# Folding w_phi into two projection weights by 120-row blocks, and copying three transposed tiles in two parts: a linear-attention and gated-MLP kernel

## The chip, the cores and the metric

The kernel runs on one core of a Trainium2 chip. The metric is the device time of one launch in microseconds (us). A core has five engines, each with its own queue that is worked in order: TensorE (PE in the profile, its weight loads PEld), VectorE (DVE), ScalarE (ACT), GpSimd (POOL) and SyncE (SP), which here only issues transfers (DMAs). TensorE writes to PSUM, eight banks of 512 fp32 columns; from there VectorE or ScalarE must copy results to SBUF. Engines wait for each other by semaphores.

## The reference

The input x has 2048 tokens of 640 features in bf16. It is layer-normalized, and the result xn feeds two branches whose outputs are added to x:

```python
xn = layernorm(x)                                   # 2048 x 640
q, k, v = split(xn @ wqkv)                          # 32 heads of 20 columns each
pq, pk  = q_h @ w_phi_h, k_h @ w_phi_h              # one 20x20 matrix per head
phi(p)  = concat(softmax(p), softmax(-p))           # 40 features per head
kv, z   = sum over tokens of phi_k x v, of phi_k
o       = (phi_q @ kv) / (phi_q . z + 1e-6)
out     = x + o @ wo + (silu(xn @ w1) * (xn @ w3)) @ w2   # w1, w3: 640 x 1536
```

## The kernel before

Tokens are worked in 16 tiles of 128, features in DC = 5 chunks of 128 partitions.

**An order made by a planner.** The code writes no order by hand. Each piece of work is a step of one of 14 streams (generators such as norms, transposes, fold_k, attention, mlps). A loop at lines 924 to 965 builds every stream's next step, asks when it could start by a table of modelled costs (`cost=` in the helpers, transfers in `commit`, lines 172 to 204), and commits the earliest. Each engine then gets its instructions in the order of commitment, and a wait for every dependency that it doesn't know to be met (`emit`). So a changed cost or size can also move steps that the edit doesn't touch. All instructions are recorded by one helper, so the profile shows them on line 102 (transfers on 114).

**The head of the program.** `first_loads` (414 to 431) issues the loads: x tiles 0 to 3 one by one, the v part of wqkv (wv), a third of w1 and w3, w_phi (phi_s), then k's part of wqkv transposed by the DMA (wqkT, one transfer of 640 rows by 640 columns), x tiles 4 to 15 in three transfers, and q's part of wqkv transposed. `consts` (434 to 443) makes the identity, zeros for idle products and the mask GM[128, 5, 32], which says for every chunk of 128 rows of w_phi (all heads stacked, 640 rows) to which head a row belongs. `consts_late` (445 to 450) makes three more constants on GpSimd after the statistics of tile 6: the mask M3 for the key-value sums, ones behind ekt, and a column of ones for every head in v2.

**Transposes.** TensorE transposes the normalized tiles 0 to 3 (`xn_transpose`, 519 to 528): five 128x128 products into PSUM, then copies to xnT. Tile 0 goes to two banks and is copied by ScalarE (three chunks) and VectorE (two). Tiles 1 to 3 go to one bank each and leave it in one copy of 640 columns, by whichever of ScalarE and VectorE the planner finds free (`evac`). Tiles 4 to 15 are transposed by DMAs. In between TensorE multiplies tiles 0 to 3 by wv: ten products of 320 columns a tile (`part`), two halves of five; the products of a tile need all its five chunks one after the other.

**The fold.** Since pq = xn (wq w_phi), the kernel multiplies w_phi into the weights once. `block_diag` (531 to 537) puts w_phi on the diagonal: for each chunk of 128 rows of w_phi it writes BDc[128, up to 8 heads x 20], one GpSimd product of 140 or 160 columns with the mask. 128 rows are 6.4 heads, so the chunks overlap in the heads at their edges. `fold_mm(which, dc, k)` (539 to 551) makes 128 rows of the folded weight Wkp (which = 1) or Wqp (0): for each chunk, the transposed weight block as the stationary operand and BDc as the moving one, split at column 320, which is where PSUM's second bank begins. That is six products for each dc, four of 140 columns and two of 80, and an evacuation of 640 columns. The five dc of k run after the first two groups of gate and up products, the five of q are strewn between the tiles 9 to 13 of attention.

**What follows.** k_tile (products with Wkp, two exponentials on ScalarE), v_tile, k_norm (VectorE sums, GpSimd scaling), the key-value sums, q_proj and its chain, `mlp` (ten products of 512 columns, tanh on ScalarE, two VectorE products) and `out_tile` at the end. PSUM banks are handed out in pairs (`banks`).

Of the kernel before, what the change touches and what calls it, by code (L numbers as in the profile page):

```python
# [9 lines left out]
D = 640  # L10
H = 32
# [9 lines left out]

ENGINES = ("PE", "ACT", "DVE", "POOL", "SP")
GRAN = 8


def heads_of_chunk(c):
    return (128 * c) // DH, (128 * c + 127) // DH


class _Op:  # L30
# [13 lines left out]
class _Program:  # L44
# [127 lines left out]
    def commit(self, ops):  # L172
        for o in ops:
            o.idx = len(self.ops)
            o.deps = self.find_deps(o)
            t = self.free[o.eng]
            for d in o.deps:
                t = max(t, d.end + (0.03 if d.eng == o.eng else 0.07))
            o.start = t
            if o.dma:  # L180
                self.free[o.eng] = t + 0.45
                if "T" == o.part:
                    self.free[o.eng] = t + (1.28 if o.cost < 5e5 else o.cost / 105e3)
                self.bus = max(self.bus, t + 0.5) + o.cost / (280e3 if o.part else 305e3)
                if o.part and o.cost > 5e5:
                    self.bus = max(self.bus, self.free[o.eng] + 1.0)
                o.end = self.bus + (1.5 if t < 1 else 1.6 if t < 3.5 or o.part and o.cost < 2e5 else 2.6)
# [62 lines left out]
def bass_parallel_sum__linear_kernel_hedgehog__glu_gated_swiglu__prompt_kernel(  # L250
# [29 lines left out]
    def new(name, shape, dtype, offset=None):  # L280
        size = mybir.dt.size(dtype)
        for n in shape[1:]:
            size *= n
        return P.sbuf(name, shape, dtype, region(size) if offset is None else offset)

    ident = new("ident", [128, 128], bf)
    GM = new("GM", [128, DC, H], bf)
    phi_s = new("phi_s", [128, DC, DH], bf)
    BDc = new("BDc", [128, DC, 8 * DH], bf)
    bst = new("bst", [128, T, 12], f32)  # L290
    mv = new("mv", [128, T, 2], f32)
    rstd = new("rstd", [128, T, 2], f32)
# [27 lines left out]
    ekt = new("ekt", [128, T * 2 * D + 48], bf, RE)  # L320
    hT3 = new("hT3", [128, FC, 512], bf, RE)
    w2_s = new("w2_s", [128, FC, D], bf, RE + 12288)
    eq = [new(f"eq{i}", [128, NG * 128], bf, (RKV, RE + 27648)[i // 2] + 2816 * (i % 2)) for i in range(4)]
    eqT = [new(f"eqT{i}", [128, NG, 128], bf, (RKV, RE + 27648)[i // 2] + 5632 + 2816 * (i % 2)) for i in range(4)]
    hT = [hT0, hT1, hT2, hT3]
# [3 lines left out]
    oT = new("oT", [128, DC, S], bf, RV)  # L329

    RW = region(12800)
    wqkT = new("wqkT", [128, 2 * DC, D], bf, RW)
    KVc = new("KVc", [128, NG * 64], bf, RW)
    half = new("half", [128, 2, 660], f32, RW + 1408)
    Sq = new("Sq", [128, 4, 72], f32, RW + 6688)
# [64 lines left out]
    x_t = A_x.rearrange("b (t p) d -> p (b t) d", p=128)  # L400
    out_t = out.rearrange("b (t p) d -> p (b t) d", p=128)
    wqkv_t = A_wqkv.rearrange("(c p) n -> p c n", p=128)
    phi_t = A_w_phi.rearrange("h d f -> (h d) f").rearrange("(c p) f -> p c f", p=128)
    w1_t = B_w1.rearrange("(c p) f -> p c f", p=128)
    w3_t = B_w3.rearrange("(c p) f -> p c f", p=128)

# [3 lines left out]

    def load_x(a, b):
        P.dma("SP", x_tok[:, a:b, :], x_t[:, a:b, :])

    def first_loads():
        def half_wv(eng, a):
            P.dma(eng, wv[:, :, a:a + 320], wqkv_t[:, :, 2 * D + a:2 * D + a + 320])

        P.dma("SP", x_tok[:, 0, 0:320], x_t[:, 0, 0:320])
        P.dma("ACT", x_tok[:, 0, 320:D], x_t[:, 0, 320:D])
        load_x(1, 2)  # L420
        load_x(2, 3)
        half_wv("ACT", 0)
        half_wv("SP", 320)
        load_x(3, 4)
        w13(0, 512)
        P.dma("SP", phi_s[:], phi_t)
        P.dma("SP", wqkT[:, DC:2 * DC, :], A_wqkv[:, D:2 * D], True)
        load_x(4, 8)
        load_x(8, 12)
        load_x(12, 16)  # L430
        P.dma("SP", wqkT[:, 0:DC, :], A_wqkv[:, 0:D], True)


    def consts():
        memset("DVE", t1[:, 2, :], 0.0)
        memset("DVE", warm[:], 0.0)
        act(warm[:], warm[:], ACT.Exp)
        memset("POOL", ident[:], 0.0)
        select(ident[:], 0, [[-1, 128]], 1, ALU.not_equal, 1.0)
        memset("POOL", GM[:], 1.0)  # L440
        select(GM[:], 0, [[128, DC], [-DH, H]], 1, ALU.is_ge, 0.0)
        select(GM[:], DH, [[-128, DC], [DH, H]], -1, ALU.is_gt, 0.0)
        memset("POOL", mhalf[:], -0.5)

    def consts_late():
        memset("POOL", M3[:, 0:3], 1.0)
        select(M3[:, 0:3], 0, [[-40, 3]], 1, ALU.is_ge, 0.0)
        select(M3[:, 0:3], 40, [[40, 3]], -1, ALU.is_gt, 0.0)
        memset("POOL", ekt[:, T * 2 * D:T * 2 * D + 48], 1.0)
        memset("POOL", v_heads(v2[:].rearrange("p t n -> p (t n)"))[:, :, :, DH], 1.0)  # L450


    def v_heads(a):
        return a.rearrange("p (g x) -> p g x", x=64)[:, :, 0:63].rearrange("p g (h c) -> p g h c", c=21)
# [58 lines left out]
    def idle(n, cols):  # L513
        z = t1[:, 2, :]
        for i in range(n):
            j = 7 - i if cols == 512 else 7
            mm(bank(j, cols), z[:, 0:128], z[:, 0:cols], True, True, cost=cols / 1200)

    def xn_transpose(t, k):
        dst = xnT[:, :, t * 128:(t + 1) * 128]  # L520
        for j, a, b in ((0, 0, 3), (1, 3, DC)) if t == 0 else ((0, 0, DC),):
            o = PSb[:, (k + j) * 1024:(k + j) * 1024 + 128 * (b - a)].rearrange("p (c n) -> p c n", n=128)
            for dc in range(a, b):
                tr(o[:, dc - a, :], x_tok[:, t, 128 * dc:128 * dc + 128])
            if t == 0:
                copy(("ACT", "DVE")[j], dst[:, a:b, :], o, 2)
            else:
                evac(dst, o)


    def block_diag():
        for c in range(DC):
            h0, h1 = heads_of_chunk(c)
            n = h1 - h0 + 1
            tt("POOL", BDc[:, c, 0:n * DH].rearrange("p (h k) -> p h k", k=DH),
               phi_s[:, c, :].unsqueeze(1).to_broadcast([128, n, DH]),
               GM[:, c, h0:h1 + 1].unsqueeze(2).to_broadcast([128, n, DH]), ALU.mult)

    def fold_mm(which, dc, k):
        first = [True, True]  # L540
        for e in range(DC):
            h0, h1 = heads_of_chunk(e)
            lo, hi = DH * h0, DH * (h1 + 1)
            for q in range(2):
                a, b = max(lo, 320 * q), min(hi, 320 * q + 320)
                if a < b:
                    mm(bank(k + q, b - a, a - 320 * q), wqkT[:, which * DC + e, 128 * dc:128 * dc + 128],
                       BDc[:, e, a - lo:b - lo], first[q], e == DC - 1 or (q == 0 and e == 2), True)
                    first[q] = False
        dst = (Wqp, Wkp)[which]  # L550
        evac(dst[:, dc, :].rearrange("p (b c) -> p b c", c=320), bank2(k, 320))


    def part(w, t, q, i, k, off=0):
# [172 lines left out]
    done = dict.fromkeys(("w", "ln", "t", "f", "k", "n", "kv", "v", "u", "qp", "qn", "qd", "q", "o", "h", "v0"), 0)  # L727

    def norms():
        yield lambda: (first_loads(), consts())  # L730
# [18 lines left out]
        yield lambda: ln_apply(3)  # L749
        done["ln"] = 4  # L750
        yield block_diag
        todo = []
        for t in range(4, T + 2, 2):
            if t == T or t > done["k"] + 8:
                for u in todo:
                    yield lambda u=u: ln_apply(u)
                    done["ln"] = u + 1
                todo = []
            if t == T:
                break  # L760
            while t > done["k"] + 8:
                yield None
            yield lambda t=t: ln_stats(t, 2)
            for u in todo:
                yield lambda u=u: ln_apply(u)
                done["ln"] = u + 1
            todo = [t, t + 1]
            if t == 6:
                yield consts_late

    def fold_k():
        for dc in range(DC):
            yield lambda dc=dc: fold_mm(1, dc, banks(2))
        done["f"] += 1
# [10 lines left out]
    def transposed(t):  # L785
        while done["ln"] <= t:
            yield None
        yield lambda: xn_transpose(t, banks(1 if t else 2))
        done["t"] = t + 1

    def transposes():
# [235 lines left out]
```

## Time and profile before

| | us |
|---|---|
| median of 3 runs | 268.59 (268.48 to 268.87) |
| the profiled execution: its time | 268.63 |
| its span, from the first to the last instruction | 266.9 |
| PE busy | 263.2 (99%) |
| DVE busy | 169.9 (64%) |
| POOL busy | 102.9 (39%) |
| ACT busy | 98.0 (37%) |

TensorE's clock is granted in full over the whole span (1.0). "Busy" says how long an engine had an instruction in work; matmuls overlap, so a busy TensorE can still be waiting for less than the length of a product. A row of the timeline gives the start, the length from the first start to the last end, the engine, the line, the instruction, what it writes and reads, its shapes and the count; in brackets stands idle time of the engine just before it and what ended it. A row with a count merges neighbours of like kind and takes its shape from the first. The chain is followed back from the last instruction, at each step to what released it.

### The profile page before, as it was taken

The numbers are of one execution on the slowest core, as the hardware profiler recorded it, in microseconds if no ns is written. First come the engines' busy times: TensorE is split into PE (matmuls) and PEld (weight loads), VectorE is DVE, ScalarE is ACT, GpSimd is POOL, SyncE is SP. The second block draws the span as 40 slices with busy tenths as digits, with TensorE's granted clock in tenths as the row PEclk, the third lists the DMA queues.
The fourth block names the chain that finished last, engine by engine and source line by source line (L and its number), as shares of the span: only waits on it lengthen the run. The fifth ranks groups of instructions, "written<-read, shape, count | busy, mean of one in ns | idle before, by whom it ended". The sixth has DMA issues, their size and how long they took to land.

```text
span 266.9 us, 4814 instructions
## 1 busy us (share of the span) xinstructions
PE 263.2 (99%) x1959; PEld 159.9 (60%) x1959; DVE 169.9 (64%) x292; ACT 98.0 (37%) x193; POOL 102.9 (39%) x144
## 2 busy tenths in 40 slices
PE   8999999999999999999999999999999999999996
PEld 4656677776754555555555544544577777777773
DVE  4559899997966779888888888988512121212112
ACT  5557989888224442443443344322100000000000
POOL 3317658999992344445555444420000000000000
DMA  7998795900095442445444553423212213131211
GB/s 214 295 315 166 178 192 111 311 1 2 6 333 64 79 79 44 92 83 101 79 81 79 97 84 78 92 50 77 49 52 74 75 54 95 52 98 49 88 37 49
DMA packets 63510, 27.73 MB, mean 104 GB/s; under 512 B 49920, under 2 KB 63488, under 8 KB 63488
## 3 DMA queue, kind: packets, MB, share of 16 engines
q1 hardware_dynamic: 62544, 26.90, 43.5%
q10 hardware_dynamic: 944, 0.52, 0.7%
q8 instruction: 15, 0.25, 0.4%
q14 instruction: 7, 0.06, 0.1%
HBM read 12.81 MB, written 2.62 MB: 58 GB/s over the span
## 4 chain that ended last, share of the span: by engine, by line
PE 98%; ACT 0%; DVE 0%; issue 0%
PE PS L102 98%; ACT xnT L102 0%; DVE xres L102 0%; DVE t L102 0%; DVE warm L102 0%
## 5 line engine op out<-in xcount | busy, mean ns | idle before, releaser
L102 PE MATMUL PS<-xnT,w_s 128*128 128x512 bf16 x480 | 107.7, 379 | 0.0
L102 PEld LDWEIGHTS PS<-xnT,w_s 128*128 128x128 bf16 x480 | 45.8, 98 | 51.0 <-ACT Wkp L102 0.2
L102 PE MATMUL PS<-w_s,hT 128*128 128x320 bf16 (+2 forms) x384 | 54.9, 299 | 0.0
L102 DVE TENSOR_TENSOR xres<-PS,xres 128x640 bf16<-128x640 f32 (+2 forms) x17 | 13.3, 785 | 59.9 <-PE PS L102 59.9
L102 ACT ACTIVATE th<-PS 128x512 f32<-128x512 f32 x48 | 29.3, 611 | 49.4 <-PE PS L102 49.4
L102 DVE SCALAR_TENSOR_TENSOR t<-th,PS 128x512 bf16<-128x512 f32 x48 | 32.5, 676 | 22.3 <-ACT th L102 22.3
L102 PEld LDWEIGHTS PS<-w_s,hT 128*128 128x128 bf16 x384 | 37.1, 98 | 15.1
L102 POOL TENSOR_TENSOR ekt<-ekt,rS 128x640 bf16<-128x640 bf16 x32 | 39.5, 1269 | 0.6 <-DVE rS L102 0.6
L102 ACT ACTIVATE eq<-PS 128x600 bf16<-128x600 f32 (+1 forms) x72 | 23.8, 424 | 29.7 <-PE PS L102 29.7
L102 DVE SCALAR_TENSOR_TENSOR hT<-t,PS 128x512 bf16<-128x512 bf16 x48 | 33.0, 687 | 1.7
L102 PE MATMUL PS<-wv,xnT 128*128 128x320 bf16 x160 | 24.5, 299 | 0.1
L102 PE MATMUL PS<-wo_s,oT 128*128 128x320 bf16 (+2 forms) x160 | 24.5, 299 | 0.0
L102 POOL TENSOR_TENSOR rq<-rq,Sq 128x32 f32<-128x32 f32 x16 | 4.0, 252 | 52.6 <-DVE rq L102 52.6
L102 PE MATMUL PS<-Wqp,xnT 128*128 128x512 bf16 (+1 forms) x160 | 24.2, 299 | 0.0
L102 PE MATMUL PS<-Wkp,xnT 128*128 128x320 bf16 x160 | 23.9, 299 | 0.0
L102 POOL TENSOR_TENSOR eq<-eq,rq 128x600 bf16<-128x600 bf16 (+1 forms) x32 | 22.6, 728 | 1.2
L102 DVE TENSOR_REDUCE S<-ekt 128x64 f32<-128x1280 bf16 x16 | 23.0, 1438 | 0.0
L102 ACT ACTIVATE ekt<-PS 128x640 bf16<-128x640 f32 x32 | 20.6, 709 | 4.8 <-PE PS L102 4.8
L102 POOL TENSOR_TENSOR half<-eq 128x660 f32<-128x660 bf16 x15 | 20.4, 1358 | 0.6 <-ACT eq L102 0.6
L102 PEld LDWEIGHTS PS<-wo_s,oT 128*128 128x128 bf16 x160 | 15.5, 98 | 6.5
L102 PEld LDWEIGHTS PS<-wv,xnT 128*128 128x128 bf16 x160 | 15.4, 98 | 6.3 <-ACT xnT L102 0.4
L102 PEld LDWEIGHTS PS<-Wqp,xnT 128*128 128x128 bf16 x160 | 12.9, 98 | 10.5
(56 smaller groups left out, 181.2 us busy)
## 6 DMA issues: line engine op xcount, KB each, us to landing
w_s<-in_B_w_dram SPq DMA_DIRECT2D x6, 640.0 KB, 6.3
xres<-in_A_x_dram SPq DMA_DIRECT2D x16, 160.0 KB, 2.5
out_dram<-xres SPq DMA_DIRECT2D x15, 160.0 KB, 1.8
x_tok<-in_A_x_dram SPq DMA_DIRECT2D x3, 640.0 KB, 6.4
w_s<-in_B_w_dram SPq DMA_DIRECT2D x1, 1920.0 KB, 8.4
wo_s<-in_A_wo_dram SPq DMA_DIRECT2D x1, 800.0 KB, 8.3
x_tok<-in_A_x_dram SPq DMA_DIRECT2D x3, 160.0 KB, 4.0
wv<-in_A_wqkv_dram ACTq DMA_DIRECT2D x1, 400.0 KB, 4.1
```

The source lines that it names most:

```text
L102: o = _Op(eng, lambda: m(*args, **kw), r, w, cost)
```

## The change

1. **The fold by heads.** w_phi and the transposed weights are cut into six blocks of whole heads: five of 120 rows (six heads) and one of 40 (two heads). Block g of k is loaded by a DMA of its own, transposing 128 columns from 640 + 120 g on, so neighbouring blocks overlap by eight columns that are not used; likewise for q. w_phi comes in two loads (600 and 40 rows). Each dc is folded by six products, five of 120 columns contracted over 120 rows and one of 40 over 40. They fill PSUM from column 32 of a pair of banks, so that four blocks end where the first bank ends, and the evacuation reads 640 columns in one piece.
2. **The masked weights** BD[128, 6, 120] are made by two GpSimd products (600 columns, 40 columns) with a mask of six columns, GM[128, 6].
3. **Tiles 1 to 3** are transposed into two banks each and leave them in two copies: ScalarE three chunks and two (tiles 1 and 2), VectorE two chunks and ScalarE three (tile 3).
4. **Constants at the head.** consts_late is gone; M3 and the ones behind ekt are made on GpSimd at the end of consts, the ones in v2 on VectorE.
5. k's blocks have a place of their own, in the region of ekt's later tiles; the planner counts a longer way to landing for small transposing loads from DRAM; fold_k waits in the planner until block_diag has been committed.

The order that the planner makes of it is, beside the edits themselves, the same on every engine up to the first gate products but for two things: eight instead of six v products stand between the transposes of tiles 1 and 2 (and 15 instead of 17 after those of tile 3), and v2's memset stands third on VectorE. From the key-value sums on, some groups of gate products stand at other places among the q tiles.

```diff
-    GM = new("GM", [128, DC, H], bf)
-    phi_s = new("phi_s", [128, DC, DH], bf)
-    BDc = new("BDc", [128, DC, 8 * DH], bf)
+    GM = new("GM", [128, 6], bf)
+    phi_s = new("phi_s", [128, 6, DH], bf)
+    BD = new("BD", [128, 6, 120], bf)
...
+    wkT = new("wkT", [128, 6, D], bf, RE + 20480)
...
-    wqkT = new("wqkT", [128, 2 * DC, D], bf, RW)
+    wqT = new("wqT", [128, 6, D], bf, RW)
...
-    phi_t = A_w_phi.rearrange("h d f -> (h d) f").rearrange("(c p) f -> p c f", p=128)
+    phi_t = A_w_phi.rearrange("h d f -> (h d) f")
...
+    def load_wT(which):
+        for g in range(6):
+            a = D * which + 120 * g
+            P.dma("SP", (wqT, wkT)[which][:, g, :], A_wqkv[:, a:a + 128], True)
...
-        P.dma("SP", phi_s[:], phi_t)
-        P.dma("SP", wqkT[:, DC:2 * DC, :], A_wqkv[:, D:2 * D], True)
+        P.dma("SP", phi_s[0:120, 0:5, :], phi_t[0:600, :].rearrange("(c p) f -> p c f", p=120))
+        P.dma("SP", phi_s[0:40, 5, :], phi_t[600:D, :])
+        load_wT(1)
         load_x(4, 8)
         load_x(8, 12)
         load_x(12, 16)
-        P.dma("SP", wqkT[:, 0:DC, :], A_wqkv[:, 0:D], True)
+        load_wT(0)
...
-        select(GM[:], 0, [[128, DC], [-DH, H]], 1, ALU.is_ge, 0.0)
-        select(GM[:], DH, [[-128, DC], [DH, H]], -1, ALU.is_gt, 0.0)
+        select(GM[:], 0, [[-DH, 6]], 1, ALU.is_ge, 0.0)
+        select(GM[:], DH, [[DH, 6]], -1, ALU.is_gt, 0.0)
         memset("POOL", mhalf[:], -0.5)
-
-    def consts_late():
+        memset("DVE", v_heads(v2[:].rearrange("p t n -> p (t n)"))[:, :, :, DH], 1.0)
         memset("POOL", M3[:, 0:3], 1.0)
         select(M3[:, 0:3], 0, [[-40, 3]], 1, ALU.is_ge, 0.0)
         select(M3[:, 0:3], 40, [[40, 3]], -1, ALU.is_gt, 0.0)
         memset("POOL", ekt[:, T * 2 * D:T * 2 * D + 48], 1.0)
-        memset("POOL", v_heads(v2[:].rearrange("p t n -> p (t n)"))[:, :, :, DH], 1.0)
...
+    PARTS = (((0, 0, 3, "ACT"), (1, 3, DC, "DVE")), ((0, 0, 3, "ACT"), (1, 3, DC, "ACT")),
+             ((0, 0, 3, "ACT"), (1, 3, DC, "ACT")), ((0, 0, 2, "DVE"), (1, 2, DC, "ACT")))
+
     def xn_transpose(t, k):
         dst = xnT[:, :, t * 128:(t + 1) * 128]
-        for j, a, b in ((0, 0, 3), (1, 3, DC)) if t == 0 else ((0, 0, DC),):
+        for j, a, b, e in PARTS[t]:
             o = PSb[:, (k + j) * 1024:(k + j) * 1024 + 128 * (b - a)].rearrange("p (c n) -> p c n", n=128)
             for dc in range(a, b):
                 tr(o[:, dc - a, :], x_tok[:, t, 128 * dc:128 * dc + 128])
-            if t == 0:
-                copy(("ACT", "DVE")[j], dst[:, a:b, :], o, 2)
-            else:
-                evac(dst, o)
+            copy(e, dst[:, a:b, :], o, 2)
...
     def block_diag():
-        for c in range(DC):
-            h0, h1 = heads_of_chunk(c)
-            n = h1 - h0 + 1
-            tt("POOL", BDc[:, c, 0:n * DH].rearrange("p (h k) -> p h k", k=DH),
-               phi_s[:, c, :].unsqueeze(1).to_broadcast([128, n, DH]),
-               GM[:, c, h0:h1 + 1].unsqueeze(2).to_broadcast([128, n, DH]), ALU.mult)
+        for n, a, b in ((120, 0, 5), (40, 5, 6)):
+            m = n // DH
+            o = BD[0:n, a:b, 0:n].rearrange("p c (h f) -> p c h f", f=DH)
+            tt("POOL", o, phi_s[0:n, a:b, :].unsqueeze(2).to_broadcast([n, b - a, m, DH]),
+               GM[0:n, 0:m].unsqueeze(1).unsqueeze(3).to_broadcast([n, b - a, m, DH]), ALU.mult)
 
     def fold_mm(which, dc, k):
-        first = [True, True]
-        for e in range(DC):
-            h0, h1 = heads_of_chunk(e)
-            lo, hi = DH * h0, DH * (h1 + 1)
-            for q in range(2):
-                a, b = max(lo, 320 * q), min(hi, 320 * q + 320)
-                if a < b:
-                    mm(bank(k + q, b - a, a - 320 * q), wqkT[:, which * DC + e, 128 * dc:128 * dc + 128],
-                       BDc[:, e, a - lo:b - lo], first[q], e == DC - 1 or (q == 0 and e == 2), True)
-                    first[q] = False
-        dst = (Wqp, Wkp)[which]
-        evac(dst[:, dc, :].rearrange("p (b c) -> p b c", c=320), bank2(k, 320))
+        c0 = k * 512 + 32
+        for g in range(6):
+            n = 120 if g < 5 else 40
+            mm(PS[:, c0 + 120 * g:c0 + 120 * g + n], (wqT, wkT)[which][0:n, g, 128 * dc:128 * dc + 128],
+               BD[0:n, g, 0:n], g in (0, 4), g in (3, 5), True)
+        evac((Wqp, Wkp)[which][:, dc, :], PS[:, c0:c0 + D])
...
-            if t == 6:
-                yield consts_late
...
-        yield lambda: xn_transpose(t, banks(1 if t else 2))
+        yield lambda: xn_transpose(t, banks(2))
```

More of the change, by code (lines that the diff above doesn't have):

```diff
@@ L23 @@
 GRAN = 8
-def heads_of_chunk(c):
-    return (128 * c) // DH, (128 * c + 127) // DH
 class _Op:
@@ L186, in commit @@
                     self.bus = max(self.bus, self.free[o.eng] + 1.0)
-                o.end = self.bus + (1.5 if t < 1 else 1.6 if t < 3.5 or o.part and o.cost < 2e5 else 2.6)
+                o.end = self.bus + (1.5 if t < 1 else 1.6 if t < 3.5 or o.part and o.cost < 2e5 and o.reads else 2.6)
             else:
@@ L725, in banks @@
         return min((k for k in range(0, 8, n) if k // 2 not in held), key=free_at)
-    done = dict.fromkeys(("w", "ln", "t", "f", "k", "n", "kv", "v", "u", "qp", "qn", "qd", "q", "o", "h", "v0"), 0)
+    done = dict.fromkeys(("w", "ln", "t", "f", "k", "n", "kv", "v", "u", "qp", "qn", "qd", "q", "o", "h", "v0", "bd"), 0)
     def norms():
@@ L751, in norms @@
         yield block_diag
+        done["bd"] = 1
         todo = []
@@ L767, in norms @@
             todo = [t, t + 1]
-            if t == 6:
-                yield consts_late
     def fold_k():
+        while not done["bd"]:
+            yield None
         for dc in range(DC):
```

## The prediction

> **What bounds the kernel now.** I read the page's span and chain shares first, then the chain in order of time, then the timeline of the places where the chain leaves TensorE.
>
> ```profile
> span 266.9 us, 4814 instructions
> PE PS L102 98%; ACT xnT L102 0%; DVE xres L102 0%; DVE t L102 0%; DVE warm L102 0%
> ```
> ```profile
> 7.52 0.47 PE PS L102 x5
> ...
> 8.01 0.71 ACT xnT L102
> 8.72 0.05 issue
> 8.77 10.90 PE PS L102 x90
> ...
> 19.67 244.91 PE PS L102 x1826
> ```
>
> The chain is TensorE's instruction stream: from 19.67 us to the end it is never left. It is left once in the stage that the change touches, at 8.01, for one ScalarE copy. So a change is worth what it takes out of TensorE's own stream, plus what it removes or adds in waits before about 20 us. Work moved on VectorE, GpSimd and SP counts only where TensorE comes to wait for it. Everything in the sum is against the profiled execution, 268.63 us (span 266.9 and 1.73 around it, which I leave alone); the median of the three runs shown is 268.59, so the two agree.
>
> **Term 1: the copies of tiles 1 to 3.** The timeline of TensorE, VectorE and ScalarE there (start, length, then the instruction and its count):
>
> ```profile
> 7.52 0.45 PE L102 MATMUL PS<-ident,x_tok 128*128 128x128 bf16 x5
> 7.81 1.27 PE L102 MATMUL PS<-wv,xnT 128*128 128x320 bf16 x6
> 8.94 0.45 PE L102 MATMUL PS<-ident,x_tok 128*128 128x128 bf16 x5
> 9.23 1.79 PE L102 MATMUL PS<-wv,xnT 128*128 128x320 bf16 x12
> 10.89 0.45 PE L102 MATMUL PS<-ident,x_tok 128*128 128x128 bf16 x5
> 11.18 2.47 PE L102 MATMUL PS<-wv,xnT 128*128 128x320 bf16 x17
> 13.49 4.48 PE L102 MATMUL PS<-xnT,w_s 128*128 128x512 bf16 x20
> ```
> ```profile
> 8.45 0.43 DVE L102 TENSOR_SCALAR x_tok<-x_tok,mv,rstd 128x640 bf16<-128x640 bf16 x1
> 10.38 0.45 DVE L102 TENSOR_SCALAR x_tok<-x_tok,mv,rstd 128x640 bf16<-128x640 bf16 x1 [0.66 <-POOL rstd L102]
> 6.11 0.49 ACT L102 ACTIVATE xnT<-PS 128x384 bf16<-128x384 bf16 x1 [0.16 <-PE PS L102]
> 8.01 0.70 ACT L102 ACTIVATE xnT<-PS 128x640 bf16<-128x640 bf16 x1 [1.41 <-PE PS L102]
> 8.69 0.72 ACT L102 ACTIVATE v<-PS 128x660 bf16<-128x660 f32 x1
> ```
>
> 17 products of 320 columns start between 11.18 and 13.49: 0.136 us each. After the transposes of tile 1, TensorE has five products of tile 0 left, 7.81 + 5 x 0.136 = 8.49. The sixth needs tile 1, whose copy ends at 8.71; it starts at 8.77, so 0.28 us are idle. Split, the first copy waits for three transposes instead of five: they start every (7.81 - 7.52)/5 = 0.06 us, so it starts about 0.11 earlier, at 7.90. It has the size of the 0.49 us row and ends at 8.39; with the 0.05 of issue, tile 1 can start at 8.44, before 8.49. The wait goes, by a margin of 0.05.
>
> What is late next is VectorE. The transposes of tile 2 need its normalization, done at 8.88, and those of tile 3 at 10.83; neither moves, so both groups stay at 8.94 and 10.89. But in the changed program eight products, not six, stand before 8.94 (8.49 + 3 x 0.136 = 8.90), and still twelve between 9.23 and 10.89. So 15 products are left after 11.18 instead of 17, and the gate products start 2 x 0.136 = **0.27 us earlier**, at 13.22.
>
> The other new copies must not be late in turn. From 384 and 640 columns (0.49, 0.70), 256 columns on ScalarE cost 0.39. Tile 1's second copy ends at 8.78 (needed after 9.23), the copy of v at 9.50, tile 2's two at 9.99 and 10.38 (needed at 9.23 + 7 x 0.136 = 10.18, and 10.59). Tile 3's last starts near 11.38 and ends at 11.87, needed at 11.18 + 7 x 0.136 = 12.13. Margins of 0.2 us: hidden. If the copies ran one after the other in the 0.70 of a whole copy each, the term would be nothing; that is its lower end.
>
> **Term 2: the fold's columns.** Sixty products of 140, 80 and 80 columns become fifty of 120 and ten of 40.
>
> ```profile
> 17.80 1.86 PE L102 MATMUL PS<-BDc,wqkT 128*128 128x140 bf16 x30
> 19.67 2.33 PE L102 MATMUL PS<-xnT,w_s 128*128 128x512 bf16 x10
> 45.73 0.48 PE L102 MATMUL PS<-BDc,wqkT 128*128 128x140 bf16 x6
> 46.05 1.52 PE L102 MATMUL PS<-Wkp,xnT 128*128 128x320 bf16 x10
> 68.48 3.96 PE L102 MATMUL PS<-v,ekt 128*128 128x63 bf16 x132
> 18.32 3.09 ACT L102 ACTIVATE Wkp<-PS 128x640 bf16<-128x640 f32 x5 [0.80 <-PE PS L102]
> ```
>
> A 512-column product takes (17.80 - 13.49)/20 = 0.2155 us and a 320-column one 0.136, so 0.000414 per column and 0.0035 over. A group before is 4 x 0.0615 + 2 x 0.0366 = 0.319; the row says 46.05 - 45.73 = 0.32. After: 5 x 0.0532 = 0.266 and one of 40 columns, which by columns would be 0.020, but 132 products of 63 and 42 columns start every 3.96/132 = 0.030 or a little less, so I take 0.029. That is 0.295, **0.024 less per group**. The five groups for q lie in the unbroken stretch: 0.12 us. The five for k are paced by ScalarE: 30 products from 17.80 end by columns at 17.80 + 5 x 0.32 = 19.40, yet the next product starts at 19.67, when ScalarE has emptied two banks. Only the first group's 0.024, before ScalarE's first copy, comes through; I count 0.03. Together **0.15 us**. Unknown is what contraction over 120 and 40 rows costs; every row here has 128. I take no difference; the ends are 0.33 gained (720 - 640 columns x 10 x 0.000414) and nothing.
>
> **Term 3: what feeds the fold.** One transposing load of 640 rows by 640 columns becomes six of 640 by 128, and w_phi comes in two loads.
>
> ```profile
> 0.80 1.34 SPq L114 DMA_DIRECT2D x_tok<-in_A_x_dram  x3
> 4.28 1.66 SPq L114 DMA_DIRECT2D phi_s<-in_A_w_phi_dram  x1
> 5.98 6.73 SPq L114 DMA_TRANSPOSE wqkT<-in_A_wqkv_dram  x1
> 12.76 1.67 SPq L114 DMA_DIRECT2D x_tok<-in_A_x_dram  x3
> 24.23 5.16 SPq L114 DMA_TRANSPOSE xnT<-x_tok  x4
> ```
> ```profile
> phi_s<-in_A_w_phi_dram SPq DMA_DIRECT2D x1, 25.0 KB, 7.8
> wqkT<-in_A_wqkv_dram SPq DMA_TRANSPOSE x1, 10.4
> xnT<-x_tok SPq DMA_TRANSPOSE x12, 2.7
> 12.00:14.00 2.00, 2.00 (x16) 1.35 (x14) 0.00 (x0) 1.03 (x2) 1.86 (x5) 1.00 1.27 290
> ```
>
> k's transposed weights land at 5.98 + 10.4 = 16.4, and the fold wants them at 17.80. After, the fold's first group wants its six blocks from 17.53 to 17.80. On SP, the second w_phi load costs about 1.34/3 = 0.45; then six issues like xnT's, which move as much each (160 KB): 5.16/4 = 1.29. The last is issued at 6.4 + 5 x 1.29 = 12.9 and lands 2.7 later, **15.6**: the early bound. The late one: w_phi lands at 12.1, and the five blocks needed 4.3 us from there; six at that rate need 5.2, **17.3**. Both are in time, by 0.5 us at the worst. The loads of x tiles 4 to 15 move from 12.76 to about 14.2; their first consumer, the statistics of tile 4, is VectorE work at 18.88, and tile 4 is first multiplied at 29.43, so I cost the shift at nothing. q's six transposes end on SP at about 14.2 + 1.7 + 7.7 = 23.6, still ahead of 24.23.
>
> **Term 4: constants.**
>
> ```profile
> 0.92 0.27 DVE L102 MEMSET t<- 128x256 uint32 x1 [0.92 <-PEq L1012]
> 3.06 0.89 DVE L102 BATCH_NORM_STATS2 bst<-x_tok 128x6 f32<-128x320 bf16 x2 [1.85 <-DMA x_tok<-in_A_x_dram]
> 4.47 0.57 POOL L102 TENSOR_TENSOR rstd<-rstd,mhalf 128x1 f32<-128x1 f32 x1 [1.87 <-DVE rstd L102]
> 12.14 1.96 POOL L102 TENSOR_TENSOR BDc<-phi_s,GM 128x140 bf16<-128x140 bf16 x5 [1.79 <-DMA phi_s<-in_A_w_phi_dram]
> 24.85 2.45 POOL L102 MEMSET v<- 128x528 bf16 x1
> ```
>
> GpSimd idles 1.87 us before 4.47, which holds the small constants (some 0.7 us, less what the 6-column mask saves against 160 columns). The 528-element memset moves to VectorE's idle 1.85 us before 3.06: by VectorE's own row 0.27 x 528/256 = 0.56; if it took GpSimd's 2.45 it would delay the first statistics by 0.6 us, the upper end. GpSimd's 2.45 and the rest at 24 us come free, and TensorE never waited for them: nothing. The masked weights take about as long as their 1.96 at 12.14 and are due at 17.53.
>
> **Sum.** 268.63 - 0.27 - 0.15 = **268.2 us**.
>
> **Rivals.** (a) *The loads come too late, and it is slower.* Speaks for it: the margin is 0.5 us at the late bound, and the new blocks start 240 bytes apart, where the old ones started 256 apart, so five of six begin off the old grid. If each packet of those five cost double, five blocks of 160 KB at half of the 290 GB/s of the row take 5 x 1.13, the sixth 0.57, and the 4.3 - 2.8 = 1.5 that is not rate stays: landing at 12.1 + 7.7 = 19.8, and TensorE waits 2.0 us at the fold: **270.2**. The same on q's blocks could push the transposes of tile 4 back and bring it to 272. It decides from a landing later than 17.8 on. Everything on TensorE is queued behind that product. Against it: no row shows that fetching, and not writing, sets the 290 GB/s, and SP's 1.29 us per block is more than a block at half rate. I give it 0.2.
>
> The Trainium skill, "DMA: Bandwidth & Descriptors", section "How a descriptor splits into AXI transactions", says that a transaction must begin on a 256-byte boundary and that the bytes ahead of the start are fetched for nothing; by it a 256-byte row at such an offset is two fetches. No row here has a transposing load off the grid.
>
> (b) *Nothing is gained.* The margin of 0.05 at 8.44 fails, ScalarE's two copies take as long as the whole one, and short contractions cost what the columns save: **268.6**. The rows of copies of 384 and 256 columns speak against it. 0.1. (c) *More is gained:* the columns' upper end (0.33) comes through as well as part of the idle time at 19.67: **267.9**. ScalarE's pace, 3.09 for five copies, speaks against it. 0.1.
>
> **How the numbers follow.** The forecast has 0.6. Its own range is 268.0 to 268.5. The three runs spread from 268.48 to 268.87, and about 0.2% (0.54 us) is what a measurement can tell from no change. Faster than 268.05: a quarter of the forecast's 0.6, and (c): 0.25. Slower than 269.1: most of (a): 0.18. Within: 0.57. The range 267.9 to 269.7 leaves out the worse part of (a) and little below.
>
> **What would show it.** In the changed profile: no ScalarE piece in the chain near 8; transposes of tiles 2 and 3 still at 8.94 and 10.89; the first gate product at 13.2; six fold products in about 0.295 at 45 us; no wait of the fold on a transposed load; the later stages merely shifted by 0.42. A TensorE gap at the fold's start that ends with a load makes (a) right and the forecast wrong; a first tile-1 product later than 8.5 breaks term 1.

## The result and the profile after

The changed kernel takes **273.23 us** (median of 5 runs, 272.55 to 273.45), the kernel before 268.59: a ratio of 1.0166, 95% interval 1.0154 to 1.0178. The forecast was 268.2 with a range up to 269.7, so it is wrong by 5.0 us and on the wrong side. The profiled execution has a span of 271.7 us against 266.9 before, at the full clock in both: 4.8 us to be found.

The page after, its first line and its shares of the chain by line:

```profile
span 271.7 us, 4803 instructions
PE PS L98 83%; SPq L110 6%; DVE bst L98 3%; DMA xnT<-x_tok 2%; DMA x_tok<-in_A_x_dram 2%; DVE x_tok L98 1%; DVE hT L98 1%; DVE S L98 1%; DVE t L98 0%; DVE mv L98 0%; DVE rS L98 0%; DVE xres L98 0%
```

Before, TensorE was 98% of the chain. Now SP's queue, two kinds of loads and VectorE's work (its statistics first) hold a sixth of it. The chain in order of time (start, length, what):

```profile
4.28 1.50 SPq L110
...
5.83 1.04 SPq L110
...
6.91 2.23 SPq L110
...
9.19 1.70 SPq L110
...
10.93 1.27 SPq L110
...
12.24 1.27 SPq L110
...
13.56 2.28 SPq L110
...
15.88 1.27 SPq L110
...
17.20 4.76 DMA x_tok<-in_A_x_dram
...
37.43 6.68 DMA xnT<-x_tok
...
44.25 24.36 PE PS L98 x190
```

The chain does not reach TensorE for good before 44.25, where it was 19.67 before. It starts as SP's issues one behind the other: two of w_phi (1.50 and 1.04) and k's six blocks, 6.91 to 17.15. Three of the blocks take 1.27, three take 1.70 to 2.28. Behind them come x tiles 4 to 7, which land at 21.96. The same on SP's timeline of the changed kernel, and below it q's load before (the row of k's, 6.73 us from 5.98, stands in the prediction):

```profile
6.91 10.24 SPq L110 DMA_TRANSPOSE wkT<-in_A_wqkv_dram  x6
18.93 10.72 SPq L110 DMA_TRANSPOSE wqT<-in_A_wqkv_dram  x6
29.70 5.24 SPq L110 DMA_TRANSPOSE xnT<-x_tok  x4
```
```profile
14.48 7.73 SPq L114 DMA_TRANSPOSE wqkT<-in_A_wqkv_dram  x1
```

k's load holds SP 3.5 us longer than before (10.24 against 6.73), q's 3.0 us (10.72 against 7.73), and tile 4's transposes, issued at 24.23 before, start at 29.70, at once behind q's last block. For tile 8's transposes (37.43) the profile alone does not decide: SP is busy until 37.39 (34.98 + 2.41, two gate weights), and VectorE, through which the chain goes, until 37.44. TensorE's timeline shows what that costs (in brackets the idle time ahead of a row and what ended it):

```profile
7.87 1.25 PE L98 MATMUL PS<-wv,xnT 128*128 128x320 bf16 x8
...
11.24 2.20 PE L98 MATMUL PS<-wv,xnT 128*128 128x320 bf16 x15
13.49 4.26 PE L98 MATMUL PS<-xnT,w_s 128*128 128x512 bf16 x19
17.59 0.43 PE L98 MATMUL PS<-BD,wkT 120*128 120x120 bf16 x5
19.15 2.14 PE L98 MATMUL PS<-BD,wkT 40*128 40x40 bf16 x25 [1.13 <-DMA wkT<-in_A_wqkv_dram]
21.45 2.11 PE L98 MATMUL PS<-xnT,w_s 128*128 128x512 bf16 x9 [0.16 <-ACT Wkp L98]
...
32.51 1.53 PE L98 MATMUL PS<-Wkp,xnT 128*128 128x320 bf16 x10 [1.37 <-DMA xnT<-x_tok]
...
44.25 1.52 PE L98 MATMUL PS<-Wkp,xnT 128*128 128x320 bf16 x10 [0.70 <-DMA xnT<-x_tok]
...
49.68 0.55 PE L98 MATMUL PS<-BD,wqT 120*128 120x120 bf16 x6
50.17 1.53 PE L98 MATMUL PS<-Wkp,xnT 128*128 128x320 bf16 x10
```

Two rows show 19 and 9 gate products where 20 and 10 are issued: the first one's record is missing (the weight loads of the second group begin at 21.22), so those groups really start one product (0.2155) earlier, at 13.27 and 21.23. With that, the account against the rows of before:

| | before | after | gain or loss |
|---|---|---|---|
| fold of k starts | 17.80 | 17.59 | -0.21 |
| from there to the next gate product | 1.87 (to 19.67) | 3.64 (to 21.23) | +1.77 |
| from there to tile 4's k product | 9.76 (to 29.43) | 11.28 (to 32.51) | +1.52 |
| from there to tile 8's | 10.87 (to 40.30) | 11.74 (to 44.25) | +0.87 |
| five fold groups of q | 0.32 each | 0.49 each | +0.85 |

The sum is 4.80, the whole difference of the spans (the 40.30 of before is this row of its TensorE timeline):

```profile
40.30 1.52 PE L102 MATMUL PS<-Wkp,xnT 128*128 128x320 bf16 x10
```

So there are two things to explain: loads that come late in three places, and fold groups that got longer although they have fewer columns.

### The profile page after: what moved, and what is told of

Read it like the earlier page. It is cut to its first block, busy times and chain, and to the rows that moved or that the text cites. A ratio compares the mean times of both kernels' runs of the same rounds, so it can differ in the third digit from the quotient of the medians.

```text
span 271.7 us, 4803 instructions
## 1 busy us (share of the span) xinstructions
PE 263.7 (97%) x1939; PEld 160.1 (59%) x1959; DVE 169.0 (62%) x293; ACT 99.2 (36%) x196; POOL 99.8 (37%) x140
## 4 chain that ended last, share of the span: by engine, by line
PE 83%; SPq 6%; DVE 6%; DMA 4%; issue 1%
PE PS L98 83%; SPq L110 6%; DVE bst L98 3%; DMA xnT<-x_tok 2%; DMA x_tok<-in_A_x_dram 2%; DVE x_tok L98 1%; DVE hT L98 1%; DVE S L98 1%; DVE t L98 0%; DVE mv L98 0%; DVE rS L98 0%; DVE xres L98 0%
## 5 line engine op out<-in xcount | busy, mean ns | idle before, releaser
L98 PE MATMUL PS<-xnT,w_s 128*128 128x512 bf16 x464 | 105.7, 379 | 1.0 <-ACT Wkp L98 0.2
L98 PE MATMUL PS<-Wqp,xnT 128*128 128x128 bf16 (+1 forms) x157 | 23.5, 298 | 0.2
L98 PEld LDWEIGHTS PS<-Wkp,xnT 128*128 128x128 bf16 x160 | 15.1, 98 | 8.7 <-DMA xnT<-x_tok 1.9
```

Of the source, the lines that this page charges most:

```text
L98: o = _Op(eng, lambda: m(*args, **kw), r, w, cost)
```

## The experiments

**The theories.** A: SP cannot issue the cut loads as fast as I took it; their lateness, and that of everything behind them in SP's order, is the three waits. B, its rival, is the mechanism of my rival (a): packets that start off the 256-byte grid are slow. C: a product over 40 rows next to products over 120 or 128 costs time at each change. D, its rival: a product of 40 columns is slow by itself. All ratios are against runs of the kernel before on the same chip:

| run | us | ratio, 95% interval |
|---|---|---|
| e1_pad_rows | 272.15 | 1.0139 (1.0121 to 1.0157) |
| e2_split_only | 268.43 | 0.9994 (0.9985 to 1.0002) |
| e3_on_grid | 272.62 | 1.0147 (1.0129 to 1.0166) |
| e4_q_later | 277.89 | 1.0345 (1.0330 to 1.0360) |
| e5_five_loads | 271.64 | 1.0144 (1.0092 to 1.0196) |
| e6_one_load | 268.25 | 0.9983 (0.9973 to 0.9992) |
| e7_rows (one time) | 273.22 | |
| e8_empty_queue (one time) | 269.68 | |
| e9_two_cut | 268.80 | 1.0005 (0.9995 to 1.0014) |
| e10_five_same | 270.02 | 1.0059 (1.0037 to 1.0082) |
| f1_q_last | 269.94 | 1.0048 (1.0032 to 1.0063) |
| f4_order | 273.85 | 1.0204 (1.0179 to 1.0230) |
| m1_mixed | 271.72 | 1.0112 (1.0096 to 1.0129) |
| m2_mixed | 268.43 | 0.9994 (0.9985 to 1.0003) |

### The rows of the sixth product: e1 and e7

```diff
-            mm(..., (wqT, wkT)[which][0:n, g, ...], BD[0:n, g, 0:n], ...)
+            mm(..., (wqT, wkT)[which][0:120, g, ...], BD[0:120, g, 0:n], ...)
+        memset("POOL", BD[:, 5, 0:40], 0.0)
```

> The changed kernel, with one thing undone: the sixth product of a fold group is contracted over 120 rows like the five before it (the rows of the mask block beyond 40 are zeros), so all six products have the same rows, and the result is the same. Theory C (going from products of 120 rows to one of 40 rows and back costs about 0.1 us each way): a group for q takes 0.295 us instead of the 0.49 of the changed kernel; five groups give 1.0 us, and k's five at most 0.7 more, because ScalarE's copies (3.1 us for five) cover some of it: 271.5 to 272.3 against 273.2. Rival D (the product of 40 columns is slow by itself): the group stays at 0.49, and the time at 273.2.

TensorE's timeline of e1:

```profile
32.39 1.53 PE L98 MATMUL PS<-Wkp,xnT 128*128 128x320 bf16 x10 [1.83 <-DMA xnT<-x_tok]
...
48.80 0.45 PE L98 MATMUL PS<-BD,wqT 120*128 120x120 bf16 x6
49.10 1.52 PE L98 MATMUL PS<-Wkp,xnT 128*128 128x320 bf16 x10
```

A group of q takes 0.30, as forecast; D falls. From the fold's start to the next gate product k's part takes 3.08 (17.56 to 20.64) instead of 3.64, so some 0.56 of the 1.77 in the table was the rows' and the rest the wait for the sixth block. What k's part gained came to nothing: TensorE arrives at tile 4 earlier and waits 1.83 there instead of 1.37, so 32.51 became only 32.39. That is why the time is near the upper end of what was expected.

Which changes of rows cost is asked of one kernel, with another row count in each group of q (the mask block filled up with zeros as in e1):

```diff
+            r = n if g < 5 else 120 if which else (40, 40, 64, 96, 97)[dc]
+            for a, b in ((0, 20), (20, 40)) if (which, dc, g) == (0, 1, 5) else ((0, n),):
+                mm(..., (wqT, wkT)[which][0:r, g, ...], BD[0:r, g, a:b], ...)
```

> The changed kernel, with the sixth product contracted over another number of rows in each fold group of q (zeros in the mask block beyond 40): 40, 40 (as two products of 20 columns), 64, 96 and 97 rows; k's over 120. The result is the same. Theory C (a price for going from 120 to 40 rows and back, not for the product): groups of 0.49, 0.52 (one product more inside the short stretch, some 0.03), then by the number of rows: if it is any change of rows, 0.49 for 64, 96 and 97; if it hangs on rows in steps of 32 (120 and 97 need four such steps, 96 three, 64 and 40 two), 0.49 for 64 and 96 and 0.295 for 97. Rival D (each short product is slow by itself): the second group takes 0.69.

Its TensorE timeline, the five groups and, for three of them, the start of what follows:

```profile
49.84 0.55 PE L98 MATMUL PS<-BD,wqT 120*128 120x120 bf16 x6
50.33 1.53 PE L98 MATMUL PS<-Wkp,xnT 128*128 128x320 bf16 x10
...
53.05 0.57 PE L98 MATMUL PS<-BD,wqT 120*128 120x120 bf16 x7
...
56.28 0.55 PE L98 MATMUL PS<-BD,wqT 120*128 120x120 bf16 x6
56.76 1.53 PE L98 MATMUL PS<-Wkp,xnT 128*128 128x320 bf16 x10
...
59.49 0.45 PE L98 MATMUL PS<-BD,wqT 120*128 120x120 bf16 x6
59.78 1.52 PE L98 MATMUL PS<-Wkp,xnT 128*128 128x320 bf16 x10
...
62.50 0.45 PE L98 MATMUL PS<-BD,wqT 120*128 120x120 bf16 x6
```

From its start to the next product's, the group with 40 rows takes 0.49, with 64 rows 0.48 and with 96 rows 0.29. By the rows' own lengths 40 rows in two products cost 0.02 more than in one (0.57 against 0.55), so the price is paid once per stretch and not per product, and D falls again; 97 rows are as short as 96 (0.45). The price is 0.2 us for one stretch of at most 64 rows among products of more than 64, and my steps of 32 rows are refuted: the bound lies between 64 and 96. The Trainium skill, "TensorEngine Tiling (Array Packing)", section "Key Properties", says that a change of the tiling mode drains TensorE, and its section "Available Configurations" has modes of 128, 64 and 32 rows. The rows agree with it if a product over 64 rows or fewer runs in such a mode, which no run here shows; the 0.2 us is this case's own measurement.

### The grid: e3

```diff
-            a = D * which + 120 * g
+            a = D * which + 128 * min(g, 4)
```

> The changed kernel, with the six transposing loads of k and of q starting at columns 0, 128, 256, 384, 512 and 512 of their part instead of 0, 120, 240, 360, 480, 600: as many loads, rows and bytes, all starting a multiple of 256 bytes into the row; the folds so get wrong columns of the weights. Theory A (SP's issuing of six loads, at 1.27 us each and more, makes them late): nothing changes; SP is through with k's six at about 17.2, the sixth lands near 19.0, TensorE waits 1.1 to 1.3 us for it, and the time is 273.2. Rival B (packets that start off the 256-byte grid cost double): the issues shrink to 1.27 each, the sixth lands before 17.3, the wait at the fold goes, the waits of tiles 4 and 8 shrink with q's loads, and the time is 270 or below.

SP's and TensorE's timelines of e3:

```profile
6.87 10.18 SPq L110 DMA_TRANSPOSE wkT<-in_A_wqkv_dram  x6
```
```profile
18.99 2.14 PE L98 MATMUL PS<-BD,wkT 40*128 40x40 bf16 x25 [0.67 <-DMA wkT<-in_A_wqkv_dram]
```

SP needs 10.18 for k's six, as off the grid (10.24), and the sixth product starts at 18.99 instead of 19.15. Nor were the DMA engines busy anything like twice as long off the grid: from 7 to 17 us their mean busy share is 0.97 in e3 and 1.02 in the changed kernel. B falls as the cause. The medians differ by 0.6 us (e3 has only two runs) and the intervals of the two ratios (1.0129 to 1.0166, 1.0154 to 1.0178) overlap, so a few tenths of a microsecond for the grid are not excluded. The Trainium skill's rule that the prediction weighed ("DMA: Bandwidth & Descriptors", section "How a descriptor splits into AXI transactions") gave rise to B; no such effect shows in these rows, and the measurement decides: at this load the bytes fetched for nothing, if they are, did not set the time.

### SP's order: e4, f1 and f4

e4 moves only q's six loads, behind tile 7's transposes:

```diff
         load_x(12, 16)
-        load_wT(0)
...
             if t == 7:
+                yield lambda: load_wT(0)
                 yield lambda: w13(512, 1024)
```

> The changed kernel, with q's six transposing loads issued by SP behind the transposes of tiles 4 to 7 instead of ahead of them. Theory A (SP's queue order hands the delay on): the transposes of tile 4 are issued as soon as its normalization is done, about 27 us instead of 29.7, and land before 30; TensorE's waits of 1.5 us for tile 4 and 0.87 us for tile 8 go, and the time is 270.8. If the waits came from the late x tiles alone (the tokens of tiles 4 to 7 landed at 22.0 instead of 18.0), the transposes stay at 32.5 and the time at 273.2. The fold's wait for the sixth block of k stays in both.

TensorE's timeline of e4 at its longest wait:

```profile
46.57 4.02 PE L98 MATMUL PS<-xnT,w_s 128*128 128x512 bf16 x10 [4.69 <-DMA w_s<-in_B_w_dram]
```

The time was missed by 7 us, because I had moved the loads ahead of the next gate weights, and those came 4.7 us late. The wait cost more than its length: the ten products behind it take 4.02 us where ten took 2.33 before, and the clock granted to TensorE, 1.00 until then, is 0.55 from 46.5 to 48.5 and 0.59 from 48.5 to 50.5. For tile 4 the mechanism did what A said: its wait is gone. Tile 8 comes only behind the long wait, so e4 says nothing of it. f1 moves q's loads behind the gate weights too, and its folds to tiles 13 to 15 (on top of e1):

> The changed kernel with 120 rows for the sixth product, and q's six transposing loads issued by SP behind everything that tiles 4 to 15 and the gate weights need; the five folds of q move to tiles 13 to 15. Theory A: tile 4's transposes are issued at about 27, no wait for tiles 4 and 8 and none for the gate weights; the wait of the fold for k's sixth block stays (0.9 us). Time 269.2 to 269.8. If the waits of tiles 4 and 8 came from the late x tiles instead of the queue's order, they stay and the time is 272.

Its only wait for a load, and SP's timeline:

```profile
PE PS L98 <- DMA wkT<-in_A_wqkv_dram: 0.7, 1, 0.7
```
```profile
26.17 5.20 SPq L110 DMA_TRANSPOSE xnT<-x_tok  x4
```

Tile 4's transposes start at 26.17 instead of 29.70 although the x tiles are hardly earlier (VectorE's first statistics of them start at 21.57, 21.99 in the changed kernel); no wait for tiles 4 and 8 is left, only that for k's sixth block. So both waits came from q's six loads in SP's queue, and not from the late tokens. 269.94 is 2.2 under e1, a little over what was expected. Putting x tiles 4 to 7 ahead of k's loads and a third gate group ahead of the fold, besides, was a miss:

> The run before this, with two more moves: x tiles 4 to 7 are loaded ahead of k's six blocks, and the third gate product group is put ahead of the fold instead of behind it, so that the fold begins near 19.8 instead of 17.6. k's sixth block lands near 19.6, x tiles 4 to 7 near 14.5. If the loss was only the lateness of these loads against TensorE's order, no wait is left and the time is 268.2 to 268.4. If TensorE needed the third gate group behind the tile 3 products as cover for tile 4's transposes, a wait of up to 1 us comes up there: 269.2.

No load is waited for any more, but the reordered VectorE and ScalarE are:

```profile
PE PS L98 <- ACT Wkp L98: 2.2, 2, 1.5
```

Here too the ten gate products behind a wait of 1.47 us take 3.69 instead of 2.33, at a granted clock of 0.50 (24.8 to 26.6) and 0.71 (26.6 to 28.4). The two moves together cost 3.9 us against f1; I did not part them.

### The cut itself: e6, e5, e10, e9 and e8

e6 has one load for k and one for q again, and e1's rows; the sixth product reads block 4:

```diff
-        for g in range(6):
-            a = D * which + 120 * g
-            P.dma("SP", (wqT, wkT)[which][:, g, :], A_wqkv[:, a:a + 128], True)
+        P.dma("SP", (wqT, wkT)[which][:, 0:5, :], A_wqkv[:, D * which:D * which + D], True)
```

> The changed kernel with both suspected costs taken out: the sixth product contracts 120 rows as in the run before, and each transposing load of k and q is one of 640 by 640 again, so that the folds get wrong columns of the weights (products of the same sizes). If the six issues and the 40 rows are the whole loss: SP is through with k's load near 13.5, x tiles 4 to 7 land by 18.6, TensorE waits for none of these loads, and the time is 268.2 to 268.3, what was forecast. If something else of the change costs as well, the time stays above that by its size.

```profile
6.88 5.58 SPq L110 DMA_TRANSPOSE wkT<-in_A_wqkv_dram  x1
...
23.94 5.17 SPq L110 DMA_TRANSPOSE xnT<-x_tok  x4
```

268.25: the whole loss is gone with the two causes, and what is left is the forecast's own sum. Nothing else of the change (two w_phi loads, constants, the two GpSimd products) costs a measurable time. In e5, the kernel before with its loads cut into five, the sixth block is missing and the starts are on the grid:

```diff
-        P.dma("SP", wqkT[:, DC:2 * DC, :], A_wqkv[:, D:2 * D], True)
+        for g in range(DC):
+            P.dma("SP", wqkT[:, DC + g, :], A_wqkv[:, D + 128 * g:D + 128 * g + 128], True)
```

> The kernel before, with each of its two transposing loads of 640 by 640 cut into five of 640 by 128 at stride 128; folds, w_phi, copies and constants as before. It parts the cutting from the sixth block. If what costs is the cutting (an issue of its own for each block, with a stall while the queues are full): SP needs about 8.9 us for k's five, like the first five of the changed kernel (2.2, 1.7, 1.3, 1.3, 2.3), instead of 6.7, x tiles 4 to 7 land at about 20 instead of 18, and TensorE waits up to 0.5 us for tile 4; time 268.6 to 269.3. If what costs is the sixth block and the second w_phi load alone: SP needs 6.4 to 6.7 us and the time is 268.6.

It came out slower than expected, 271.64, but the planner had also put the fold two microseconds earlier, because it counts short loads as landing sooner. e10 cuts the same loads with every other instruction in the order of before, and e9 cuts them in two:

> The kernel before with each transposing load cut into five of 128 columns and every other instruction of every engine in the same order, the fold at 17.8 too. If cutting alone costs SP its time: k's five take 8.9 to 9.4 us instead of 6.7 and land by 17.2, in time for the fold; q's five end at 27 instead of 22.2, tile 4's transposes are issued there instead of at 24.2 and land near 30, and TensorE waits 0.5 to 0.8 us for them: 269.1 to 269.5. If the earlier run with five loads was slow only by its other order: 268.6.

> The kernel before with each transposing load cut in two (256 and 384 columns) and every other instruction of every engine in the same order. If the cost of cutting grows with the number of loads: SP needs 7.2 to 7.6 us for k's (6.7 in one piece, 9.4 in five), q's 8.0 to 8.5, and the time stays at 268.6, as tile 4's transposes begin at 24.2 in the kernel before whatever SP did until then. If a single cut already costs what four do: 9.4 and, with q's behind it, 269 to 270.

SP's timelines, e10 first, then e9:

```profile
6.52 9.64 SPq L419 DMA_TRANSPOSE wqkT<-in_A_wqkv_dram  x5
...
17.93 9.24 SPq L419 DMA_TRANSPOSE wqkT<-in_A_wqkv_dram  x5
27.21 5.43 SPq L114 DMA_TRANSPOSE xnT<-x_tok  x4
```
```profile
6.05 6.71 SPq L114 DMA_TRANSPOSE wqkT<-in_A_wqkv_dram  x2
...
14.79 8.66 SPq L114 DMA_TRANSPOSE wqkT<-in_A_wqkv_dram  x2
```

For the same bytes SP is held 6.73 and 7.73 us in one piece, 6.71 and 8.66 in two, 9.64 and 9.24 in five. Cutting alone, with no sixth block, off no grid and in no other order, delays tile 4's transposes to 27.21 and costs time (a ratio of 1.0059, somewhat more than I expected). Of the 1.0 us by which e10's profiled span is longer, TensorE's rows put 0.36 ahead of tile 4 and 0.29 ahead of tile 8; another 0.32 is there when the fold starts (18.12 against 17.80), before any cut load is used. Two pieces cost nothing measurable, and for k not even time on SP. So what counts in A is how finely the load is cut; whether by the number of issues or by their width (128 columns against 256 and more) these runs do not part. Whether each issue is long because loads ahead of it are unfinished was asked with q's six loads at the end, with the last gate weights ahead of them (f1) or behind them (e8):

> The run with q's blocks last, with the last two gate weight loads (655 KB each) issued behind q's six blocks instead of ahead of them. It is for the length of SP's issues. If a transposing issue takes longer while loads ahead of it wait in the queues: behind the gate weights the six took 1.35, 1.67, 1.82, 1.76, 1.27 and 1.27 us, 9.35 from first to last, and here they take 1.27 to 1.35 each, 7.7 to 8.0 in all. If the length belongs to these loads (off the grid, from HBM): 9.3 again. The time is not the point; the gate weights land later, which may add a wait.

```profile
46.36 9.35 SPq L110 DMA_TRANSPOSE wqT<-in_A_wqkv_dram  x6
```
```profile
45.82 8.79 SPq L110 DMA_TRANSPOSE wqT<-in_A_wqkv_dram  x6
```

f1 first, then e8: 9.35 and 8.79. In e8 five of the six took 1.27 to 1.28 and one 2.21, with nothing bulky ahead; in f1 four took 1.35 to 1.82. By these two single executions the backlog explains some 0.6 us of the stretch, but not the single long issue. Nor is it a flood of bytes: from 13.5 to 15.8, during k's longest issue in the changed kernel (2.28), all DMAs together moved 74 GB/s. What SP waits for in a long issue stays open.

### The copies, and what can be kept: e2, m1 and m2

e2 gives the kernel before the PARTS of the change and two banks for tiles 1 to 3, and nothing else.

> The kernel before with term 1 alone (two copies for each of tiles 1 to 3 on the engines of the changed kernel; folds, loads and constants as before). If term 1 is right: TensorE does 8 instead of 6 products of v between the transposes of tiles 1 and 2, the first gate product starts at 13.22 instead of 13.49, and the time is 268.3. If the constants or the other edits had made this gain in the changed kernel: 13.49 and 268.6.

```profile
8.26 0.45 PE L102 MATMUL PS<-ident,x_tok 128*128 128x128 bf16 x5 [0.33 <-DVE x_tok L102]
8.54 1.25 PE L102 MATMUL PS<-wv,xnT 128*128 128x320 bf16 x8
...
13.94 4.48 PE L102 MATMUL PS<-xnT,w_s 128*128 128x512 bf16 x20
```

In this execution x tile 1 came late and all of the head with it, but from tile 1's transposes to the first gate product it is 5.68 us (13.94 - 8.26), where before it was 13.49 - 7.52 = 5.97: 0.29 less, with eight products in the row, as forecast. The median is 0.32 lower; the interval still touches 1. m1 and m2 add q's fold by 120 columns (with 120 rows) to it, and leave k's as before:

```diff
-        load_wT(1)
+        P.dma("SP", wkT[:, 0:DC, :], A_wqkv[:, D:2 * D], True)
...
-                yield lambda dc=dc: fold_mm(1, dc, banks(2))
+                yield lambda dc=dc: fold_k_mm(dc, banks(2))   # the products of before
...
         yield lambda: w13(1024, 1536)
+        yield lambda: load_wT(0)
```

> A version that keeps of the change only what paid: split copies; k as in the kernel before (one transposing load, 128-row blocks, 60 products' worth of columns); q by six blocks of 120 with 120 rows in the sixth product, its loads on SP behind tile 15's transposes and its folds at tiles 13 to 15. Expected: 0.27 from the copies and 0.12 from q's columns, 268.2 against 268.6, a ratio near 0.9985. If q's six late issues or the second mask block put something else late, 268.6 or more.

GpSimd's timeline of m1:

```profile
21.49 1.39 POOL L98 TENSOR_TENSOR BD<-phi_s,GM 120x600 bf16<-120x600 bf16 x2 [7.80 <-DMA phi_s<-in_A_w_phi_dram]
```

I had put q's w_phi rows behind 1.9 MB of x tiles, and GpSimd stood for them. The planner, which orders the steps by its modelled times, put other work ahead of tile 4's normalization: its statistics start on VectorE at 22.83 (18.88 before), behind two copies of the fold and two products of a gate group, and GpSimd, through with BD at 22.88, waits another 1.94 us for them. Tile 4's transposes and TensorE were late in turn, 271.72. With those rows loaded earlier the statistics start at 19.05:

> The mixed version again, with the w_phi rows for q's mask block loaded right behind those for k's, ahead of k's load, instead of behind the x tiles (where they landed at 21.4 us and held GpSimd). Expected: tile 4's transposes issued by 25 again, no wait for tiles 4 and 8, q's blocks landed before 58, and so 0.27 from the copies and 0.12 from q's columns: 268.2 to 268.3, a ratio near 0.9985. If GpSimd's second mask block (1.4 us) or the two more w_phi issues still push tile 4's normalization back: 269.5 or more.

m2 waits for no load in the profile and takes 268.43, a ratio of 0.9994 (0.9985 to 1.0003): the 0.12 for q's columns is not to be seen beside e2. No version that computes the reference was shown to beat the kernel before; e6, which does by 0.0017, uses wrong columns.

## Why the prediction was wrong

**Term 1, the copies: right.** The wait at 8.49 to 8.77 is gone, 8 and 15 products stand where they were put, the first gate product starts at 13.27 (forecast 13.22, with the whole head 0.06 later; 13.21 to 13.24 in e1, e3 and e6), and e2 shows 0.29 from the copies alone.

**Term 2, the columns: the sum right, a bound wrong.** With 120 rows a group takes 0.30, as worked out (0.295). The step that failed is "I take no difference; the ends are 0.33 gained ... and nothing": both ends lay on the side of a gain, though no row excluded a loss. The measured price is 0.2 us a group, 0.85 to 1.0 us on q's five.

**Term 3, what feeds the fold: the step that lost the rest.** "Six issues like xnT's, which move as much each (160 KB): 5.16/4 = 1.29" took its price from issues at 24 us, which read from SBUF; k's six, which read from DRAM at 7 to 17 us, took 1.27 to 2.28 and 10.24 us in all, where 7.7 was counted. The second w_phi load added 0.88 to SP's time (1.50 + 1.04 against 1.66), where 0.45 was counted. The early bound of 15.6 and the late one of 17.3 both failed: the sixth block was issued at 15.88 instead of 12.9 and landed 3.1 us later, and TensorE's next product started at 19.15. The late bound had been made from the rate of the data alone, with no term for a longer issue, and so was no bound.

**"So I cost the shift at nothing"** failed in the same way: x tiles 4 to 7 landed at 21.96, and q's transposes ended on SP at 29.65 instead of 23.6, "still ahead of 24.23", which made 1.52 and 0.87 us of loss on TensorE. I had seen that margin of 0.6 us and given it no price outside rival (a)'s double fetches, although q's six issues are priced by the same 1.29 as k's; it was worth more than the fold's. By medians, f1 (q's loads out of the way, its folds later) took 2.2 us off e1.

**The rivals.** Rival (a) had the place and the sign: a wait at the fold for a transposed load, then tile 4. Its mechanism, double fetches, is refuted as the cause by e3, so its place and sign came out by another mechanism than the one it named, and its 270.2 to 272 fell short of 273.2. **Term 4**: e6 shows that the constants cost nothing measurable; that v2's memset ran at 3.07 us instead of right behind the first two, delaying the head by 0.06, was not followed.

## What to carry to other kernels

Price an issue on a DMA queue by a row of the same kind of load in the same stretch of the queue, count how many issues a cut makes, and follow the queue's order to the last instruction behind them: here the loss at tiles 4 and 8, which the change does not touch, was larger than at the fold. One large transposing load cut into five cost the queue's engine 1.5 to 3 us even when bytes and order stay the same, and in two nothing that showed in the time. When a matmul's contraction is cut short and its neighbours are long, keep it at 96 rows or more, or pad it with zeros: 64 rows still paid here, and nothing between 64 and 96 was measured. A load that comes very late can cost more than TensorE's wait: in e4 a wait of 4.7 us was followed by 1.7 us of slower products.

## What was not expected of the hardware

- A stretch of products over 40 or 64 rows among products over 120 and 128 costs 0.2 us once, whether it is one product or two; over 96 or 97 rows it costs nothing (0.29 us a group against 0.49 and 0.48).
- An issue of a 160 KB transposing load from DRAM took SP 1.26 us at the least (in f4; 1.27 in the others). In five pieces 640 by 640 took 9.2 to 9.6 us of SP in e10 and 9.4 and 10.2 in e5, in one 5.6 to 7.8, though the bytes are the same.
- Starting 240 bytes apart instead of 256 changed neither SP's time for k's six (10.24 us against 10.18) nor, by more than 0.2 us, when TensorE got the sixth.
- Behind a wait of 4.69 us (e4) ten products of 512 columns took 4.02 us instead of 2.33, at a granted clock of 0.55 to 0.59; behind several waits, the last of 1.47 (f4), 3.69. Behind the single wait of 1.37 us for tile 4 in the changed kernel the clock stayed at 1.00 (33 to 36 us).
